# Multiplies behind evictions, loads ordered by need, and a second product in four banks: a fused attention and feed-forward kernel

## The chip, the cores and the metric

The kernel runs on one core of one Trainium2 chip. The metric is the device time of one execution in microseconds, and each kernel has several. An execution counts as slow if it takes over 1.5% longer than the fastest of the same kernel; only fast ones are compared in ratios. The *granted clock* is the mean TensorE clock that the profile records for an execution, 1.00 being full speed. An *eviction* is VectorE's copy of a finished bank of outputs to a buffer, from which a *store* takes it to memory; a *row tile* is 128 tokens of a group.

## The reference, cut to what matters

```python
# q, k, v: [8 batches, 8 heads, 576, 64]
k_p = k.reshape(B, H, 72, 8, D).mean(axis=3)          # 576 rows pooled to 72
v_p = v.reshape(B, H, 72, 8, D).mean(axis=3)
attn = softmax(q @ k_p.T / sqrt(D))
x = (attn @ v_p) -> [4608 tokens, 512]                 # heads side by side
h = x @ w_in                                           # 512 -> 2048, "first product"
out = gelu_tanh(h) @ w_out                             # 2048 -> 512, "second product"
```

The 4608 tokens are done in nine groups of 512. While group g is in its second product, the attention of batch g+1 is worked in between its matmuls.

## The kernel before: the parts that the argument touches

Every product goes to `PS`, eight banks of 512 f32 per partition. Outputs pass through `osb`, a pool of three buffers.

```python
opool = ctx.enter_context(tc.tile_pool(name="op", bufs=3))
PS = psp.tile([128, 8, 512], F32, name="PS")
...
load_k(0, 0, nc.sync)          # the first batch: k and v from SyncE, q from GpSimd
load_k(0, 1, nc.sync)
load_v(0, 0, nc.sync)
load_v(0, 1, nc.sync)
load_q(0, 0)
load_q(0, 1)
...                            # then w_in, batch 1, w_out, all from GpSimd
```

Normalising a head pair takes a logarithm and an exponential on ScalarE and then one or two multiplies on VectorE. The multiplies are issued at once after the exponential, so that they take their place in VectorE's order there:

```python
def norm(b, c, pr, bank):
    ...                        # ld = Ln(sum of the exponentials)
    nc.scalar.activation(out=rc, in_=ld, func=ACT.Exp, scale=-1.0)
    for x in range(2 if b else 1):
        ...
        nc.vector.tensor_tensor(out=xT[rows, pr, col:col + CH], in0=PS[rows, bank + x, :CH],
                                in1=rc[rows], op=ALU.mult)
```

A group: first product with GELU block by block, then the second product, with the next batch's attention steps at fixed places of its 64 matmuls. Two row tiles take turns on banks 0 and 1. In group 0 the order goes by pairs of row tiles, because `w_out` arrives in quarters:

```python
HB = (0, 2, 3, 1)                               # banks of the first product's blocks
...
at = (6, 14, 20, 27, 34, 41, 48, 55, 61)        # places of the attention steps
...                                             # each: score, value, exponential, norm
if g:
    seq = [(r, fo) for r in range(4) for fo in range(FO)]
else:
    for rp in range(2):
        for f4 in range(4):
            seq += [(2 * rp + x, 4 * f4 + f) for x in range(2) for f in range(4)]
for m, (r, fo) in enumerate(seq):
    if m in inserts:
        inserts[m]()
    op = PS[:, r % 2, :]
    nc.tensor.matmul(out=op, lhsT=gT[:, fo, r * 128:(r + 1) * 128], rhs=w_out_b[:, fo, :], ...)
    if fo < FO - 1:
        continue
    osb = opool.tile([128, DM], F32, name="osb")
    nc.vector.tensor_copy(out=osb, in_=op)      # the eviction
    ...                                         # the store, from SyncE
```

The softmax here doesn't subtract the row's maximum and nothing guards it: scores larger than these inputs give would overflow.

Of the kernel before, what the change touches and what calls it, by code (L numbers as in the profile page):

```python
# [8 lines left out]
F32 = mybir.dt.float32  # L9
BF16 = mybir.dt.bfloat16  # L10
ALU = mybir.AluOpType
ACT = mybir.ActivationFunctionType
# [6 lines left out]
def kernel(  # L19
# [9 lines left out]
    nc = tc.nc  # L29
    B, H, S, D = q.shape  # L30
    Sp = S // 8
    N = B * S
    DM = H * D
    DF = moe_w_in.shape[1]
    KO = DM // 128
    FO = DF // 128
    T = S // 32
# [23 lines left out]

    ks, vs, qs = {}, {}, {}

    def load_k(b, hf, eng):
        if b not in ks:
            ks[b] = kvp.tile([KP, 2, KR, 512], F32, name="kt")
        eng.dma_start(
            out=ks[b][:, hf],
            in_=k[b, hf * 4:(hf + 1) * 4].rearrange("h (j r l) d -> (h j) r (l d)", r=KR, l=8))

    def load_v(b, hf, eng):
        if b not in vs:
            vs[b] = kvp.tile([Sp, H, 512], F32, name="vt")
        eng.dma_start(  # L74
            out=vs[b][:, hf * 4:(hf + 1) * 4],
            in_=v[b, hf * 4:(hf + 1) * 4].rearrange("h (j l) d -> j h (l d)", l=8))

    def load_q(b, i):
        if b not in qs:
            qs[b] = qp.tile([128, 2, T * D], BF16, name="qb")  # L80
        nc.gpsimd.dma_start(  # L81
            out=qs[b][:, i],
            in_=q[b, i * 4:(i + 1) * 4].rearrange("h (p t) d -> (h p) (t d)", t=T))

    def load_batch(b):
        for i in range(2):
            load_q(b, i)
        for hf in range(2):
            load_k(b, hf, nc.gpsimd)
        for hf in range(2):  # L90
            load_v(b, hf, nc.gpsimd)

    w_in_b = consts.tile([128, KO, DF], BF16, name="w_in_b")
    w_out_b = consts.tile([128, FO, DM], BF16, name="w_out_b")
# [1 line left out]
    w_out_v = moe_w_out.rearrange("(fo p) d -> p fo d", p=128)  # L96
    identb = consts.tile([128, 128], BF16, name="identb")

    load_k(0, 0, nc.sync)
    load_k(0, 1, nc.sync)  # L100
    load_v(0, 0, nc.sync)
    load_v(0, 1, nc.sync)
    load_q(0, 0)
    load_q(0, 1)
    make_identity(nc, identb)
    for i in range(4):
        nc.gpsimd.dma_start(out=w_in_b[:, :, i * 512:(i + 1) * 512], in_=w_in_v[:, :, i * 512:(i + 1) * 512])

# [86 lines left out]
    def qk(b, c, pr, bank):  # L195
        for e in range(2):
            h = 2 * pr + e
            nc.tensor.matmul(out=PS[:Sp, bank + e, :CH], lhsT=kTs[b % 2][:, c, h, :],  # L198
                             rhs=qTs[b][:, h // 4, h % 4].rearrange("p c t -> p (c t)"),
                             start=True, stop=True)  # L200
# [9 lines left out]
    def av(b, c, pr, bank):  # L210
# [4 lines left out]
        for x in range(2):  # L215
# [3 lines left out]
            else:  # L219
                for y in range(2):  # L220
                    w = vz[:, pr, y] if x else ones[:, y]
                    nc.tensor.matmul(out=PS[:, bank + 1 - x, :CH], lhsT=flat(w), rhs=e[:, y, :],  # L222
                                     start=(y == 0), stop=(y == 1))

    def norm(b, c, pr, bank):
        ld = ep.tile([128, CH], F32, name="ld")
        if b:
            nc.scalar.activation(out=ld[0:64], in_=PS[64:128, bank, :CH], func=ACT.Ln)  # L228
            nc.scalar.activation(out=ld[64:128], in_=PS[0:64, bank + 1, :CH], func=ACT.Ln)  # L229
        else:  # L230
            nc.scalar.activation(out=ld, in_=PS[:, bank + 1, :CH], func=ACT.Ln)
        rc = ep.tile([128, CH], F32, name="rc")
        nc.scalar.activation(out=rc, in_=ld, func=ACT.Exp, scale=-1.0)  # L233
        col = b * S + c * CH
        for x in range(2 if b else 1):
            rows = slice(x * 64, (x + 1) * 64) if b else slice(0, 128)
            nc.vector.tensor_tensor(out=xT[rows, pr, col:col + CH], in0=PS[rows, bank + x, :CH],  # L237
                                    in1=rc[rows], op=ALU.mult)
# [3 lines left out]
    def act_set(name):  # L242
        nc.scalar.preload_act_table_set(name)  # L243


    act_set(EXP_SET)
    for s in k_steps(0, 0):
        s()
    trans_k(0, 0, 4)
    trans_q(0, *QG[0], 5, nc.scalar)  # L250
    trans_q(0, *QG[1], 6, nc.scalar)
    for s in k_steps(0, 1):
        s()
    qk(0, 0, 0, 2), expo(0, 0, 0, 2)
    qk(0, 0, 1, 0), expo(0, 0, 1, 0)
    trans_k(0, 1, 7)
    trans_q(0, *QG[2], 4, nc.vector)
    trans_q(0, *QG[3], 5, nc.vector)
    qk(0, 1, 0, 2), expo(0, 1, 0, 2)
    qk(0, 1, 1, 0), expo(0, 1, 1, 0)  # L260
    for hf in range(2):
        for s in v_steps(0, hf):
            s()
    for c in range(2):
        for pr in (2, 3):
            bank = (2, 0)[pr % 2]
            qk(0, c, pr, bank), expo(0, c, pr, bank)
    for i, (c, pr) in enumerate(ORDER):
        bank = (4, 6, 0, 2, 4, 6, 4, 6)[i]
        av(0, c, pr, bank)  # L270
        norm(0, c, pr, bank)


    HB = (0, 2, 3, 1)
    for g in range(NG):
        r0 = g * GROUP
        nb = g + 1 if g + 1 < B else None
        act_set(GELU_SET)
        if g + 2 < B:
            load_batch(g + 2)  # L280


        side = {fo: [] for fo in range(FO)}
        if nb is not None:
            k0, k1 = k_steps(nb, 0), k_steps(nb, 1)
            v0, v1 = v_steps(nb, 0), v_steps(nb, 1)
            tq = [lambda a=a, i=i: trans_q(nb, *a, 4 + i, nc.vector) for i, a in enumerate(QG)]
            tk = [lambda hf=hf: trans_k(nb, hf, 4 + hf) for hf in range(2)]
            if g:
                plan = {2: k0[:2], 3: k0[2:], 4: tq[:1], 5: [k1[0], tq[1]], 6: k1[1:] + [tq[2]],  # L290
                        7: tq[3:], 9: tk, 10: v0[:1], 11: v0[1:], 12: v1[:1], 13: v1[1:]}
            else:
                plan = {8: tq[:1], 9: [tq[1]], 10: [tq[2]], 11: tq[3:] + k0 + k1, 14: tk,
                        15: v0 + v1}
            for fo, what in plan.items():
                side[fo] += what

        gT = gpool.tile([128, FO, GROUP], BF16, name="gT")

        def p1_mm(fo, ko, c0, c1):  # L300
            nc.tensor.matmul(out=PS[:, HB[fo % 4], c0:c1], lhsT=w_in_b[:, ko, fo * 128:(fo + 1) * 128],  # L301
                             rhs=xT[:, ko, r0 + c0:r0 + c1], start=(ko == 0), stop=(ko == KO - 1))

        def gelu(fo):
            nc.scalar.activation(out=gT[:, fo, :], in_=PS[:, HB[fo % 4], :], func=ACT.Gelu_apprx_tanh)  # L305
            for s in side[fo]:
                s()


        for c0, c1 in ([(0, CH), (CH, GROUP)] if g == 0 else [(0, GROUP)]):  # L310
            for ko in range(KO):
                for fo in range(4):
                    p1_mm(fo, ko, c0, c1)
        for fo in range(4):
            gelu(fo)
        for fo in range(4, FO):
            for ko in range(KO):
                p1_mm(fo, ko, 0, GROUP)
            gelu(fo)


        inserts = {}
        if nb is not None:
            act_set(EXP_SET)
            at = (6, 14, 20, 27, 34, 41, 48, 55, 61)
            for i in range(len(ORDER) + 1):
                def step(i=i):
                    if i < len(ORDER):
                        qk(nb, *ORDER[i], 2)
                    if i:  # L330
                        av(nb, *ORDER[i - 1], 4 + 2 * ((i - 1) % 2))
                    if i < len(ORDER):
                        expo(nb, *ORDER[i], 2)
                    if i:
                        norm(nb, *ORDER[i - 1], 4 + 2 * ((i - 1) % 2))
                inserts[at[i]] = step
        if g:
            seq = [(r, fo) for r in range(4) for fo in range(FO)]
        else:
            seq = []  # L340
            for rp in range(2):
                for f4 in range(4):
                    seq += [(2 * rp + x, 4 * f4 + f) for x in range(2) for f in range(4)]
        for m, (r, fo) in enumerate(seq):
            if m in inserts:
                inserts[m]()
            op = PS[:, r % 2, :]
            nc.tensor.matmul(out=op, lhsT=gT[:, fo, r * 128:(r + 1) * 128], rhs=w_out_b[:, fo, :],  # L348
                             start=(fo == 0), stop=(fo == FO - 1))
            if fo < FO - 1:  # L350
                continue
            osb = opool.tile([128, DM], F32, name="osb")
            nc.vector.tensor_copy(out=osb, in_=op)  # L353
            c0, c1 = r0 + r * 128, r0 + (r + 1) * 128
            while c0 < c1:
                n = min(c1, (c0 // CH + 1) * CH) - c0
                b, c = divmod(c0, S)
                nc.sync.dma_start(
                    out=out[b * S:(b + 1) * S].rearrange("(j e) d -> e j d", e=2)[c // CH, c % CH:c % CH + n],
                    in_=osb[c0 - r0 - r * 128:c0 - r0 - r * 128 + n, :])  # L360
                c0 += n


# [28 lines left out]
```

## Time and profile before

| | before |
|---|---|
| time, median of 3 runs | 351.21 us (350.79 to 351.3) |
| profiled span, granted clock | 348.0 us, 0.958 |
| TensorE busy | 310.6 us |
| TensorE's first product waiting for output evictions | 14.3 us, in 8 waits |
| first GELU starts | 29.77 us |
| group 0's second product | 44.04 to about 66.5 us |

The prediction shows the lines behind most of these. Two more views matter later. The first is busy time by stretch, for the first two slices of 8.7 us; the columns are the stretch, its length, the busy time and number of instructions of TensorE, its weight loads, VectorE, ScalarE and GpSimd, the granted clock, the share of the DMA engines and what they moved in GB/s.

```profile
0.00:8.70 8.70, 0.42 (x3) 0.21 (x3) 3.93 (x10) 1.28 (x1) 7.58 (x16) 1.00 0.82 209
8.70:17.40 8.70, 6.13 (x40) 4.50 (x40) 6.99 (x14) 5.58 (x10) 2.94 (x6) 1.00 1.16 252
```

With both issuers at work, the second slice moved 252 GB/s. The second view is the output stores issued between 50 and 90 us, and the time from issue to landing.

```profile
L358 SPq DMA_DIRECT2D out_dram<-osb x5: 341/368/422, 55.5 to 69.5; - x5
...
DMA to landing us min/median/max: 6.9/8.7/11.5
```

Over the whole kernel the larger group of stores has a median of 2.0 us from issue to landing. Around the end of group 0, where the loads of later batches are in flight, it is 8.7.

### The profile page before, as it was taken

The page shows a single profiled execution, that of the slowest core. Times are in us where ns is not written, and L with a number is a line of the kernel's source. Part 1 is how long each engine was busy: PE and PEld are TensorE (multiplying, and loading weights), DVE is VectorE, ACT ScalarE, POOL GpSimd, SP SyncE. Part 2 cuts the span into 40 slices and gives each one's busy share as a digit, 9 for nine tenths or more (in the row PEclk, how much of TensorE's full clock was granted, in tenths as well). Part 3 has the DMA queues.
Part 4 walks back from the last instruction along what each step waited for, and adds up shares of the span by engine and source line. Part 5 has one row for each costly group of instructions (what it writes and reads, how often), then busy time and mean ns, then how long its engine had stood idle before and what let it go on. Part 6 is the DMA issues. An engine that isn't in the chain of part 4 may idle for free.

```text
span 348.0 us, 4327 instructions
## 1 busy us (share of the span) xinstructions
PE 310.6 (89%) x1601; PEld 157.5 (45%) x1632; DVE 182.5 (52%) x336; ACT 221.6 (64%) x411; POOL 37.0 (11%) x62
## 2 busy tenths in 40 slices
PE   0789897799997999799979997999799979999995
PEld 0555453344553555355535553545354534444442
DVE  4860884558364846584657567575667560020011
ACT  1684474846894689668946796669857985603600
POOL 8332222002100210021002100000000000000000
PEclk9978998989998999999989999899999998999998
DMA  8999999967720583158412851001100110012011
GB/s 209 252 227 223 222 208 177 250 198 176 177 79 32 121 183 127 32 107 184 119 52 40 206 157 61 1 2 44 47 32 0 30 62 30 0 61 62 0 49 72
DMA packets 17228, 37.50 MB, mean 108 GB/s; under 512 B 2328, under 2 KB 6424, under 8 KB 17208
## 3 DMA queue, kind: packets, MB, share of 16 engines
q0 software_dynamic: 11008, 25.44, 34.9%
q1 hardware_dynamic: 6200, 11.80, 10.5%
q8 instruction: 12, 0.20, 0.2%
q14 instruction: 8, 0.07, 0.1%
HBM read 36.70 MB, written 9.44 MB: 133 GB/s over the span
## 4 chain that ended last, share of the span: by engine, by line
PE 80%; DVE 8%; ACT 7%; DMA 2%; issue 1%; DVEq 0%; ACTq 0%; POOLq 0%
PE PS L301 37%; PE PS L348 32%; PE PS L198 4%; PE PS L217 3%; PE PS L181 3%; DVE xT L237 2%; DMA qb<-in_q_dram 2%; DVE osb L353 2%; ACT ld L229 2%; ACT rc L233 2%; ACT e L204 2%; ACT ld L228 1%; DVE vt L138 1%; PE PS L222 1%; DVE kt L138 1%
## 5 line engine op out<-in xcount | busy, mean ns | idle before, releaser
L301 PE MATMUL PS<-xT,w_in_b 128*128 128x512 bf16 (+2 forms) x575 | 143.5, 396 | 15.9 <-DVE osb L353 14.3
L348 PE MATMUL PS<-w_out_b,gT 128*128 128x512 bf16 x562 | 135.2, 381 | 2.9 <-DVE osb L353 2.4
L305 ACT ACTIVATE gT<-PS 128x512 bf16<-128x512 f32 x144 | 82.3, 600 | 81.2 <-PE PS L301 80.1
L301 PEld LDWEIGHTS <-w_in_b 128*128 128x128 bf16 x592 | 59.5, 103 | 83.1 <-issue 30.5
L237 DVE TENSOR_TENSOR xT<-PS,rc 64x288 bf16<-64x288 f32 (+1 forms) x120 | 54.5, 455 | 63.6 <-ACT rc L233 37.4
L348 PEld LDWEIGHTS <-gT 128*128 128x128 bf16 x576 | 56.4, 98 | 60.2 <-issue 4.3
L353 DVE COPY osb<-PS 128x512 f32<-128x512 f32 x36 | 24.8, 692 | 53.1 <-PE PS L348 52.3
L204 ACT ACTIVATE e<-PS 72x576 bf16<-72x576 f32 x64 | 40.8, 645 | 13.8 <-PE PS L198 13.0
L188 DVE COPY qT<-PS 128x640 bf16<-128x640 bf16 (+1 forms) x30 | 22.4, 765 | 31.8 <-PE PS L181 31.7
L138 DVE TENSOR_TENSOR vt<-vt 72x1024 f32<-72x1024 f32 (+1 forms) x32 | 30.5, 952 | 0.8
L233 ACT ACTIVATE rc<-ld 128x288 f32<-128x288 f32 x64 | 28.3, 442 | 2.5 <-DVE xT L237 0.5
L198 PE MATMUL PS<-qT,kT 128*72 128x288 bf16 x128 | 26.8, 298 | 2.5 <-ACT qT L186 1.0
L138 DVE TENSOR_TENSOR kt<-kt 96x768 f32<-96x768 f32 (+1 forms) x32 | 24.0, 749 | 3.7 <-DMA kt<-in_k_dram 3.1
L228 ACT ACTIVATE ld<-PS 64x288 f32<-64x288 f32 x56 | 22.8, 408 | 1.4
L229 ACT ACTIVATE ld<-PS 64x288 f32<-64x288 f32 x56 | 22.5, 402 | 1.4
L217 PE MATMUL PS<-e,vp 72*128 72x288 bf16 x112 | 23.3, 288 | 0.0
L243 ACT ACT_TABLE_LOAD x17 | 21.8, 1283 | 1.0 <-PEq L376 0.7
L198 PEld LDWEIGHTS <-kT 128*72 128x72 bf16 x128 | 14.8, 117 | 16.0 <-issue 2.4
L81 POOL DMA_DIRECT2D qb<-in_q_dram x16 | 9.2, 581 | 106.0 <-PE PS L181 95.2
L171 DVE COPY kT<-PS 64x288 bf16<-64x288 bf16 x32 | 14.4, 450 | 6.5 <-PE PS L168 6.0
L74 POOL DMA_DIRECT2D vt<-in_v_dram x14 | 10.5, 756 | 40.1 <-DVE vp L138 25.8
L181 PEld LDWEIGHTS <-qb 128*128 128x128 bf16 x144 | 11.2, 104 | 7.6 <-DMA qb<-in_q_dram 1.0
(32 smaller groups left out, 80.9 us busy)
## 6 DMA issues: line engine op xcount, KB each, us to landing
kt<-in_k_dram POOLq DMA_DIRECT2D x14, 576.0 KB, 9.0
vt<-in_v_dram POOLq DMA_DIRECT2D x14, 576.0 KB, 8.6
out_dram<-osb SPq DMA_DIRECT2D x24, 256.0 KB, 2.0
qb<-in_q_dram POOLq DMA_DIRECT2D x16, 288.0 KB, 7.0
w_in_b<-in_moe_w_in_dram POOLq DMA_DIRECT2D x4, 512.0 KB, 16.0
w_out_b<-in_moe_w_out_dram POOLq DMA_DIRECT2D x4, 512.0 KB, 20.9
out_dram<-osb SPq DMA_DIRECT2D x8, 192.0 KB, 2.2
kt<-in_k_dram SPq DMA_DIRECT2D x2, 576.0 KB, 5.9
```

Source lines behind the costliest of these rows:

```text
L138: nc.vector.tensor_tensor(out=o, in0=a, in1=b, op=ALU.add)
L198: nc.tensor.matmul(out=PS[:Sp, bank + e, :CH], lhsT=kTs[b % 2][:, c, h, :], rhs=qTs[b][:, h // 4, h % 4].rearrange("p c t -> p (c t)"), st ...
L204: nc.scalar.activation(out=e, in_=PS[:Sp, bank:bank + 2, :CH], func=ACT.Exp, scale=1.0 / 64.0)
L217: nc.tensor.matmul(out=PS[:, bank + x, :CH], lhsT=flat(vps[b % 2][:, pr, x]), rhs=e[:, x, :], start=True, stop=True)
L228: nc.scalar.activation(out=ld[0:64], in_=PS[64:128, bank, :CH], func=ACT.Ln)
L229: nc.scalar.activation(out=ld[64:128], in_=PS[0:64, bank + 1, :CH], func=ACT.Ln)
L233: nc.scalar.activation(out=rc, in_=ld, func=ACT.Exp, scale=-1.0)
L237: nc.vector.tensor_tensor(out=xT[rows, pr, col:col + CH], in0=PS[rows, bank + x, :CH], in1=rc[rows], op=ALU.mult)
L301: nc.tensor.matmul(out=PS[:, HB[fo % 4], c0:c1], lhsT=w_in_b[:, ko, fo * 128:(fo + 1) * 128], rhs=xT[:, ko, r0 + c0:r0 + c1], start=(ko == ...
L305: nc.scalar.activation(out=gT[:, fo, :], in_=PS[:, HB[fo % 4], :], func=ACT.Gelu_apprx_tanh)
L348: nc.tensor.matmul(out=op, lhsT=gT[:, fo, r * 128:(r + 1) * 128], rhs=w_out_b[:, fo, :], start=(fo == 0), stop=(fo == FO - 1))
L353: nc.vector.tensor_copy(out=osb, in_=op)
```

## The change

Its intent: (1) an eviction should not stand in VectorE's order behind a multiply that is not ready, and the bank that is evicted last should be needed last; (2) the first batch's loads go in one queue in the order of need; (3) 16 half-width matmuls of group 0's first product fill gaps of its attention; (4) group 0's second product keeps four row tiles in four banks and goes by quarters of `w_out`, so that the last quarter is needed late, with all eight score steps of batch 1 moved ahead of it.

The core of the diff. Cut are helpers, renamings and three smaller parts: groups 1 to 8 take the first matmuls in an order that touches the late bank after six of them; in group 0 the sums of batch 1's k come before the transposes of its q; ScalarE and VectorE take the first batch's four copies of q in another turn.

```diff
-    load_k(0, 0, nc.sync)
-    load_k(0, 1, nc.sync)
-    load_v(0, 0, nc.sync)
-    load_v(0, 1, nc.sync)
-    load_q(0, 0)
-    load_q(0, 1)
+    load_k(0, nc.sync, 0, 1)
+    load_q(0, 0, 1)                 # GpSimd, as all that follow
+    load_k(0, nc.gpsimd, 1, 2)
+    load_q(0, 1, 2)
     make_identity(nc, identb)
+    load_v(0, 0, 4)
+    load_v(0, 4, 8)
...
     def load_batch(b):              # later batches: k, q, v, one DMA each
+        load_k(b, nc.gpsimd)
+        load_q(b)
+        load_v(b)
...
+    def h_bank(g, fo):              # x, y change places from group to group
+        x, y = x_bank(g), 1 - x_bank(g)
+        if fo == 4:
+            return 7
+        return (x, 2, 3, y)[fo if fo < 4 else (fo - 1) % 4]
+    def o_bank(g, r):
+        if g == 0:
+            return (1, 0, 2, 3)[r]
+        return 1 - x_bank(g) if r % 2 == 0 else x_bank(g)
...
+    take = (0, 0, 0, 0, 0, 4, 6, 6)          # first-product matmuls drawn forward
     for i, (c, pr) in enumerate(ORDER):
         av(0, c, pr, bank)
         norm(0, c, pr, bank)
+        mult(0, c, pr, bank)
+        for fo, ko in early[:take[i]]:
+            p1_mm(0, fo, ko, 0, CH)
...
             if g:                            # groups 1 to 7
+                        at(pos[i], norm, *a)
+                        at(min(pos[i] + 9, 65), mult, *a)   # 65: after the last eviction
+            else:
+                for c, pr in ORDER:
+                    scores(nb, c, pr)        # all before the second product
+                for i in range(len(ORDER)):
+                    at(8 + 6 * i, av, *a)
+                    at(8 + 6 * i, norm, *a)
+                    at(min(8 + 6 * i + 8, 65), mult, *a)
...
         else:
-            for rp in range(2):
-                for f4 in range(4):
-                    seq += [(2 * rp + x, 4 * f4 + f) for x in range(2) for f in range(4)]
+            seq = [(r, 4 * f4 + f) for f4 in range(4) for r in range(4) for f in range(4)]
```

## The prediction

> **What bounds the kernel now.** I read the page's busy line and costliest groups first, then the waits, then the stages (busy time by stretch), then the order of time at one group boundary, and last the granted clock in 1 us slices.
>
> The page's first part and its costliest row (the last field is idle time just before, and who ended it):
>
> ```profile
> PE 310.6 (89%) x1601; PEld 157.5 (45%) x1632; DVE 182.5 (52%) x336; ACT 221.6 (64%) x411; POOL 37.0 (11%) x62
> L301 PE MATMUL PS<-xT,w_in_b 128*128 128x512 bf16 (+2 forms) x575 | 143.5, 396 | 15.9 <-DVE osb L353 14.3
> ```
>
> TensorE sets the end. Its own first-product matmuls wait 14.3 us for VectorE's output evictions, eight times. VectorE is half idle, so this is order, not load. The order of time at the boundary from group 2 to group 3:
>
> ```profile
> 139.61 0.81 PE L348 MATMUL PS<-w_out_b,gT 128*128 128x512 bf16 x3
> ...
> 140.26 0.81 PE L301 MATMUL PS<-xT,w_in_b 128*128 128x512 bf16 x3
> ...
> 140.89 0.44 ACT L233 ACTIVATE rc<-ld 128x288 f32<-128x288 f32 x1
> ...
> 141.37 0.94 DVE L237 TENSOR_TENSOR xT<-PS,rc 64x288 bf16<-64x288 f32 x2 [0.39 <-ACT rc L233]
> 142.34 0.69 DVE L353 COPY osb<-PS 128x512 f32<-128x512 f32 x1
> ...
> 143.09 2.96 PE L301 MATMUL PS<-xT,w_in_b 128*128 128x512 bf16 x13 [2.02 <-DVE osb L353]
> ```
>
> The last second-product matmul is issued by 140.26, but its bank's eviction stands behind two multiplies (0.94 us), which stand behind the reciprocal. The fourth matmul of the next group needs that bank, so TensorE stands for 2.02 us. The stages:
>
> ```profile
> core 0: us, PE busy (x) PEld busy (x) DVE busy (x) ACT busy (x) POOL busy (x), PEclk, DMA share, GB/s
> 24.10:44.00 19.90, 17.74 (x103) 10.09 (x104) 8.17 (x15) 10.45 (x18) 5.15 (x8) 0.88 1.13 226
> 44.00:69.50 25.50, 20.73 (x99) 10.31 (x100) 15.38 (x31) 18.31 (x35) 4.45 (x7) 0.93 1.05 210
> 106.40:143.10 36.70, 34.52 (x182) 17.53 (x185) 22.90 (x43) 26.72 (x50) 3.69 (x6) 0.95 0.44 111
> 143.10:178.30 35.20, 32.93 (x181) 17.08 (x184) 22.89 (x43) 26.73 (x50) 3.70 (x6) 1.00 0.48 114
> ```
>
> Two steady groups of the same work: 36.70 us at clock 0.95, 35.20 at 1.00. The slices after the boundary at 106.4 show where the other 1.5 us went:
>
> ```profile
> 107.00:108.00 1.00, 1.00 (x4) 0.40 (x3) 0.93 (x3) 0.00 (x0) 0.00 (x0) 0.59 0.65 246
> 108.00:109.00 1.00, 1.00 (x4) 0.30 (x2) 0.29 (x1) 0.00 (x0) 0.00 (x0) 0.50 0.06 16
> 109.00:110.00 1.00, 1.00 (x4) 0.45 (x3) 0.00 (x0) 0.00 (x0) 0.00 (x0) 0.50 0.06 12
> ```
>
> So a stall is often followed by 3.4 us at half clock: 0.43 us per matmul instead of 0.216. Five such stretches (from 69.6, 107.3, 178.9, 216.5 and 288.1) follow the boundaries; the stalls ending at 143.1 and 251.8 brought none. Group 0 has two further waits, and the start waits for the first half of q (in the chain that ended last, as start, duration, what):
>
> ```profile
> 1.26 7.73 DMA qb<-in_q_dram
> 9.04 0.73 PE PS L181 x5
> ```
>
> ```profile
> 43.03 0.30 PE L168 MATMUL PS<-identb,kp 96*128 96x96 bf16 x3 [1.54 <-DVE kp L138]
> 55.49 0.59 PE L348 MATMUL PS<-w_out_b,gT 128*128 128x512 bf16 x2 [2.44 <-DVE osb L353]
> 67.79 0.81 PE L301 MATMUL PS<-xT,w_in_b 128*128 128x512 bf16 x3 [1.33 <-DVE osb L353]
> ```
>
> **What the Trainium skill says.** "TensorE: Matmul & The Clock Gate", section "What's actually happening": the array's clock is halved after an idle window of about 3.4 us and restored after a busy one, on a free-running window. The trace agrees on the length (3.4 us) and the factor (0.50), but shows that a 2.0 us stall suffices if it lies inside one window: 104.4 to 106.4 was punished, 141.1 to 143.1 was not. The slow stretches begin at multiples of about 3.41 us from one another (107.3 to 178.9 is 21 of them), so which stalls are punished is phase. "Advanced Engine Details and Errata", section "Sequencer Loop": an instruction waits in its engine's queue for its semaphores; the same-order effect is seen above, with the ready eviction 2 us behind a multiply that is not ready. "Perfetto Trace Analysis", section "Matmuls": independent groups should rotate through PSUM banks so that evictions overlap matmuls. Here the next group's fourth matmul takes the bank evicted last, and the 2.02 us show it. "DMA: Bandwidth & Descriptors", section "Issuing engines are not separate DMA queues": all issuers share the same 16 DMA engines. The trace agrees: q took 7.73 us beside k and v from the other queue, against a minimum of 4.0 us from issue to landing for q in this trace.
>
> **The change part by part.**
>
> *Multiplies behind evictions, other bank order (groups 1 to 8).* Same instructions. The last eviction now starts about 0.2 us after the last second-product matmul and takes 0.69, as at 315.86 where no multiply is in front and TensorE resumes 0.95 us after its last issue. The late bank is now touched after six matmuls, 6 x 0.216 = 1.3 us, so the 2.02 us wait goes. The two multiply pairs end about 1.86 and 2.8 us after the product's end; the fifth output block uses bank 7, needed at 16 x 0.216 = 3.45 us, so they don't bind. Groups 2 and 3 read these last columns of xT after 8 and 12 matmuls (1.72, 2.6 us): up to 0.25 us each. A steady group becomes 35.20 - 2.02 = 33.2 us; check: 128 x 0.2155 + 16 pairs of score and value matmuls x 0.245 + 1.3 of transposes = 32.8. Groups 1 to 6 took 217.5 us (69.5 to 287.0): 217.5 - 6 x 33.2 = 18.3 saved, of which about 12 are stalls and the rest half clock. Group 7: 29.6 becomes 27.7 (half clock 1.7, and a 0.3 us wait): 1.9. Group 8: the waits at 317 and 319 go, as bank 7 is free: about 0.5.
>
> *Start.* With v no longer beside it, q's first half should land at about 5.5 to 6.5 instead of 9.0. Transposes then begin about 1.3 us earlier, behind k. But VectorE has one more q copy (0.72) and the same v sums, which still begin near 14.5 (14.91 before), so the last normalisation moves by only about 0.3 us. The real gain is 16 half-width matmuls of group 0's first product drawn into the gaps: before, 32 of them took 24.12 to 30.0, mostly at half clock. I put the first GELU at 26.5 instead of 29.77: 3.3.
>
> *Group 0's middle.* k is summed earlier, which takes away the 1.54 us wait. But all eight score pairs now stand before the second product, and the product's first bank is one of theirs. From the first product's end at about 38.2 (26.5 + 48 x 0.2155 + 1.3): the table load of 1.28 ends about 39.6, eight exponentials x 0.65 = 5.2, so the second product starts at about 44.8, 0.8 us later than before (44.04). TensorE has only 2 us of work in those 6.6, so I expect one half-clock stretch, 1.7 lost. Then 64 x 0.2155 + 8 x 0.245 + 1.7 = 17.5: end at 62.4 against 66.5 before. The stretch is shorter because the score matmuls (8 x 0.245) and the 2.44 us wait no longer lie in it. w_out is no bound: its last quarter landed about 48 (issue 27.4 + 20.9) and is needed 48 positions in, near 58.
>
> *Sum.* Group 0 ends at 62.4; then 6 x 33.2 + 27.7 + 27.6 + 4.0 (last eviction and store, 344.0 to 348.0, unchanged) = 258.5; with 0.4 for groups 2 and 3, 321.3 of span. The timed median is 3.2 us above the profiled span (351.2 against 348.0): 324.5.
>
> **The rivals.** *A new wait in the old one's place:* the next group now waits for the multiplies (bank 7, last columns of xT). Against: the end times above; for: a margin of only 0.65 us at bank 7, and none in groups 2 and 3. If 1 us stayed at each of seven boundaries, about 331; if half clock also stayed, 338 or more. *Group 0 as a new bubble:* the exponentials serialise scores for over 6 us and cost two half-clock stretches, or w_out comes later; about 4 us more, 328. *Loads hidden anyway, or late in one queue:* v behind k and q might reach VectorE after 14.5. By bytes (2.36 MB at 0.25 MB/us from 1.5 us) it lands at about 11 and 14, so at most 1 us is lost: 325.5. *Better than thought:* the clock stays up at start and in group 0: 3 to 4 us less, 321.
>
> **Range and chances.** The steady part (about 20.7 of the 26.7 us) rests on a measured group without stalls, so most uncertainty is in group 0: 324.5, range 319 to 331. Faster by over 2% (below 344.2) needs under a third of the steady gain: 0.97. Within 2%: 0.02. Slower: 0.01, some overlooked serialisation.
>
> **What would show it right or wrong.** The wait of the first product for the output eviction falls from 14.3 us to under 2; steady groups last 33 to 33.5 us at clock 0.99 or more; eight exponentials stand in a row at 39 to 45 with TensorE mostly idle and one slow stretch after; the first GELU stands at 26 to 28; group 0's second product ends between 61 and 65. The prediction is wrong if the boundaries keep a wait above 0.5 us (for a multiply or a GELU), if slow stretches appear inside dense groups, or if the second product of group 0 waits for w_out.

## The result, and the profile after

| | before | after |
|---|---|---|
| time, median of 4 runs | 351.0 us (349.75 to 351.3) | 337.27 us (334.9 to 338.08) |
| ratio of fast runs | | 0.960 (95%: 0.955 to 0.966) |
| profiled span, granted clock | 348.0 us, 0.958 | 336.2 us, 0.968 |

Ratios here and below are the mean time of one kernel's fast runs over that of the other's of the same rounds, so not quite the ratio of the medians quoted. The change is faster by 4%, but the time is 12.8 us above the predicted 324.5 and outside its range.

The profile's first part and the row of the first product, after:

```profile
PE 302.5 (90%) x1601; PEld 155.5 (46%) x1632; DVE 183.0 (54%) x336; ACT 221.2 (66%) x411; POOL 28.7 (9%) x44
...
L265 PE MATMUL PS<-xT,w_in_b 128*128 128x512 bf16 (+2 forms) x575 | 134.2, 379 | 12.2 <-DVE osb L279 11.2
```

The wait for output evictions is 11.2 us where it was 14.3. Read alone, this row says that the change hardly worked. But it was eight waits and is now two, both at one place. First, a steady boundary in order of time, from group 2 to group 3. Each line has start and length in us, engine, line, operation, what is written and read, and the count; brackets give how long the engine was idle before, and what released it.

```profile
144.39 0.81 PE L274 MATMUL PS<-w_out_b,gT 128*128 128x512 bf16 x3
145.04 3.23 PE L265 MATMUL PS<-xT,w_in_b 128*128 128x512 bf16 x13
145.24 0.69 DVE L279 COPY osb<-PS 128x512 f32<-128x512 f32 x1 [1.49 <-PE PS L274]
145.67 0.44 ACT L230 ACTIVATE rc<-ld 128x288 f32<-128x288 f32 x1
145.96 1.88 DVE L238 TENSOR_TENSOR xT<-PS,rc 64x288 bf16<-64x288 f32 x4
```

This is the aim of the change: the eviction starts 0.20 us after the next group's first matmul, the multiplies stand behind it, and 13 matmuls of the next group run without a pause. Now the stages, with the columns of the slices above (group 0's second product, group 1, group 2):

```profile
49.91:65.70 15.79, 15.69 (x78) 7.76 (x80) 8.90 (x19) 11.31 (x25) 0.84 (x1) 1.00 1.11 183
65.70:111.94 46.24, 34.84 (x183) 17.50 (x185) 22.68 (x41) 24.45 (x47) 2.20 (x3) 0.89 0.77 175
111.94:145.04 33.10, 32.88 (x182) 17.10 (x185) 22.90 (x42) 26.71 (x51) 2.20 (x3) 1.00 0.50 122
```

A steady group takes 33.10 us at clock 1.00. Group 1, the same work, takes 46.24 at 0.89, yet its TensorE is busy only 34.84: some 11 us are idle. The order of time where group 0 ends and group 1 begins:

```profile
63.31 0.69 DVE L279 COPY osb<-PS 128x512 f32<-128x512 f32 x1 [1.36 <-PE PS L274]
...
64.03 14.86 SPq L285 DMA_DIRECT2D out_dram<-osb  x5
...
64.99 0.69 DVE L279 COPY osb<-PS 128x512 f32<-128x512 f32 x1
...
66.67 0.69 DVE L279 COPY osb<-PS 128x512 f32<-128x512 f32 x1
67.42 1.24 PE L265 MATMUL PS<-xT,w_in_b 128*128 128x512 bf16 x5 [1.34 <-DVE osb L279]
77.82 0.69 DVE L279 COPY osb<-PS 128x512 f32<-128x512 f32 x1 [10.46 <-DMA out_dram<-osb]
...
78.57 5.01 PE L265 MATMUL PS<-xT,w_in_b 128*128 128x512 bf16 x14 [9.91 <-DVE osb L279]
```

Read the brackets backwards. TensorE stood for 9.91 us until the eviction at 77.82, which stood for 10.46 us until an **output store** had landed. Four row tiles in four banks all finish within the last quarter, so four evictions come in a row, and there are three `osb` buffers. The fourth eviction needs the first one's buffer, whose store was issued at 64.03. The chain that ended last has that store as one piece, and the view of the stores issued between 50 and 90 us shows that it is no exception:

```profile
64.03 13.67 DMA out_dram<-osb
```

```profile
DMA to landing us min/median/max: 8.0/13.7/15.0
```

A store is 128 x 512 x 4 bytes, 0.26 MB. In these 13.67 us the DMA engines moved 184 GB/s, some 2.5 MB, at a busy share of 1.03: they are full of loads for later batches, of which batch 3's were issued from 46.55 to 52.41. The kernel before had slow stores there too (8.7 us median), but its pairs of row tiles gave two evictions at a time, and none of them had to wait for a buffer.

At the start, the loads by slices, the chain's first piece of work, and the line where VectorE begins to sum v:

```profile
0.00:8.70 8.70, 1.03 (x9) 0.82 (x10) 4.39 (x11) 1.28 (x1) 6.59 (x15) 1.00 0.79 189
8.70:17.40 8.70, 5.95 (x35) 3.59 (x33) 5.37 (x8) 5.94 (x10) 5.83 (x8) 1.00 1.10 199
```

```profile
1.26 6.79 DMA qb<-in_q_dram
```

```profile
16.23 1.95 DVE L133 TENSOR_TENSOR vt<-vt 72x1024 f32<-72x1024 f32 x2 [1.43 <-DMA vt<-in_v_dram]
```

The first half of q lands only 0.94 us sooner than before (6.79 against 7.73), 199 GB/s are moved with nearly all loads from one issuer where two issuers moved 252, and v now holds VectorE up until 16.23, where the sums began at 14.91 before without waiting. The next load is later still: q of batch 1, which group 0's first product transposes between its last blocks. Its piece in the chain that ended last, and the transposes that wait for it:

```profile
12.96 26.75 DMA qb<-in_q_dram
```

```profile
39.76 0.45 PE L176 MATMUL PS<-identb,qb 128*128 128x128 bf16 x5 [1.04 <-DMA qb<-in_q_dram]
```

The chain goes through this load and not through the first GELU: an earlier first GELU alone would only have made TensorE wait longer here.

Where the time is, by the prediction's own terms (each end of a stage as predicted and as in the trace, in us):

| stage | predicted | measured | off by | off in sum |
|---|---|---|---|---|
| first GELU | 26.5 | 30.70 | +4.2 | +4.2 |
| group 0's first product ends | 38.2 | 43.40 | +1.0 | +5.2 |
| second product starts | 44.8 | 49.91 | -0.1 | +5.1 |
| second product ends | 62.4 | 65.70 | -1.8 | +3.3 |
| group 1 takes | 33.2 | 46.24 | +13.0 | +16.3 |
| groups 2 to 6 take | 166.4 | 164.71 | -1.7 | +14.7 |
| group 7 takes | 27.7 | 27.63 | -0.1 | +14.6 |
| group 8 and the last store | 31.6 | 31.9 | +0.3 | +14.9 |

Group 1's row has the prediction's steady group, and 166.4 is 5 x 33.2 and the 0.4 for groups 2 and 3. The sum is the difference of the spans, 336.2 against 321.3. The row of the first product's end is set by q of batch 1, as said above, whatever the row before it shows. Of group 1's 13.0 us, 9.91 are the wait for the buffer, 1.34 an eviction of group 0 that still stands behind two multiplies (64.04 and 65.71) and the rest, some 1.7, half clock: the idle stretch brought the clock down from about 72 to 82.4, and the matmuls from 78.57 to 82.4 ran at 0.43 us each instead of 0.216.

### The profile page after: what moved, and what is told of

Same layout as the page of the kernel before. It is cut to its first block, busy times and chain, and to the rows that moved or that the text cites. A ratio compares the mean times of both kernels' runs of the same rounds, so it can differ in the third digit from the quotient of the medians.

```text
span 336.2 us, 4281 instructions
## 1 busy us (share of the span) xinstructions
PE 302.5 (90%) x1601; PEld 155.5 (46%) x1632; DVE 183.0 (54%) x336; ACT 221.2 (66%) x411; POOL 28.7 (9%) x44
## 4 chain that ended last, share of the span: by engine, by line
PE 76%; DMA 14%; ACT 5%; POOL 1%; issue 1%; DVE 1%; DVEq 0%; POOLq 0%
PE PS L265 34%; PE PS L274 33%; DMA qb<-in_q_dram 10%; DMA out_dram<-osb 4%; PE PS L212 4%; PE PS L193 3%; ACT e L199 2%; PE PS L176 2%; ACT ld L226 1%; ACT ld L225 1%; DVE osb L279 1%; ACT rc L230 1%; PE PS L163 0%; ACT L244 0%; POOL kT L120 0%
## 5 line engine op out<-in xcount | busy, mean ns | idle before, releaser
L265 PE MATMUL PS<-xT,w_in_b 128*128 128x512 bf16 (+2 forms) x575 | 134.2, 379 | 12.2 <-DVE osb L279 11.2
L274 PE MATMUL PS<-w_out_b,gT 128*128 128x512 bf16 x562 | 133.7, 379 | 1.2 <-ACT e L199 0.7
L265 PEld LDWEIGHTS <-w_in_b 128*128 128x128 bf16 x592 | 57.2, 99 | 72.7 <-issue 15.3
L183 DVE COPY qT<-PS 128x512 bf16<-128x512 bf16 (+1 forms) x30 | 22.4, 762 | 7.0 <-PE PS L176 6.8
L193 PEld LDWEIGHTS <-kT 128*72 128x72 bf16 x128 | 14.6, 116 | 18.3 <-issue 3.3
L176 PE MATMUL PS<-identb,qb 128*128 128x128 bf16 x144 | 13.9, 231 | 1.4 <-DMA qb<-in_q_dram 1.4
L176 PEld LDWEIGHTS <-qb 128*128 128x128 bf16 x144 | 11.2, 104 | 8.5 <-DMA qb<-in_q_dram 2.1
L68 POOL DMA_DIRECT2D kt<-in_k_dram x8 | 5.1, 634 | 112.0 <-DVE kp L133 104.3
## 6 DMA issues: line engine op xcount, KB each, us to landing
qb<-in_q_dram POOLq DMA_DIRECT2D x7, 576.0 KB, 11.2
```

Of the source, the lines that this page charges most:

```text
L176: nc.tensor.transpose(out=half_bank(bank)[:, x * 128:(x + 1) * 128], in_=qs[b][:, i, (t0 + x) * 128:(t0 + x + 1) * 128], identity=identb)
L193: nc.tensor.matmul(out=PS[:Sp, bank + e, :CH], lhsT=kTs[b % 2][:, c, h, :], rhs=qTs[b][:, h // 4, h % 4].rearrange("p c t -> p (c t)"), st ...
L265: nc.tensor.matmul(out=PS[:, h_bank(g, fo), c0:c1], lhsT=w_in_b[:, ko, fo * 128:(fo + 1) * 128], rhs=xT[:, ko, r0 + c0:r0 + c1], start=(ko ...
L274: nc.tensor.matmul(out=PS[:, o_bank(g, r), :], lhsT=gTs[g][:, fo, r * 128:(r + 1) * 128], rhs=w_out_b[:, fo, :], start=(fo == 0), stop=(fo ...
```

## The experiments

Two questions: is the buffer the cause of group 1's length, and what is the cause of the start's? Each expectation says which theory it speaks for, by letters; A is the theory of the buffers just told. Twelve kernels ran, in four batches, each batch on one chip; all gave correct results. The edits shown leave out helper parameters. The kernel before has medians of 349.5 to 349.9 in these batches, but single runs from 343.4 (granted clock 0.99) to 352.1 (0.95). As the fastest run sets the mark, many runs of before count as slow in three of the batches, and the verdicts of the first batch are unclear, presumably for that reason, in spite of their intervals. Differences between versions are therefore read from their own runs, which mostly agree within 3 us (four runs each, six of g2 and g3).

| run | median us (lowest to highest) | ratio to before (95%) |
|---|---|---|
| e1_four_out | 326.05 (324.43 to 329.03) | 0.943 (0.928 to 0.959) |
| e2_pairs | 333.45 (330.73 to 337.2, one slow) | 0.961 (0.944 to 0.978) |
| e3_v_sync | 328.19 (327.15 to 329.34) | 0.949 (0.939 to 0.958) |
| e4_steady_only | 327.43 (326.9 to 328.03) | 0.946 (0.937 to 0.955) |
| f1_filler | 328.7 (327.68 to 328.99) | no interval |
| f2_no_early | 328.16 (327.21 to 329.38) | no interval |
| f3_old_loads | 327.44 (326.86 to 328.7) | no interval |
| f4_steady_g0 | 323.27 (323.06 to 323.41) | no interval |
| g1_hold | 329.95 (327.25 to 334.83, one slow) | 0.941 (0.935 to 0.948) |
| g2_f4_four_out | 322.64 (321.52 to 323.85) | 0.923 (0.919 to 0.928) |
| g3_best_filler | 321.01 (320.04 to 322.25) | 0.918 (0.914 to 0.923) |
| h1_loads_filler | 322.72 (322.08 to 322.98) | no interval |

### Is it the buffer? e1_four_out

The kernel after, with one more output buffer and nothing else.

```diff
-    opool = ctx.enter_context(tc.tile_pool(name="op", bufs=3))
+    opool = ctx.enter_context(tc.tile_pool(name="op", bufs=4))
```

> The changed kernel with four output buffers instead of three, nothing else. Theory A (the fourth store of group 0 has no free output buffer until the first store, 13.7 us in flight, lands): VectorE's wait for the output store (10.5 us) goes, the 9.9 us wait of TensorE and the half clock after it (1.6 us) go: about 326 us. Rival B (the evictions are late because the multiplies and evictions stand in the wrong order in group 0, and the buffer is only what the profile names last): the wait moves to a multiply or an eviction and the time stays above 333.

Measured: 326.05 us, 11.2 below the kernel after. The same place in order of time:

```profile
66.64 1.29 DVE L279 COPY osb<-PS 128x512 f32<-128x512 f32 x2
67.38 2.97 PE L265 MATMUL PS<-xT,w_in_b 128*128 128x512 bf16 x13 [1.33 <-DVE osb L279]
```

The third and fourth evictions run one after the other (x2, 1.29 us), the wait for a store is gone, and only the 1.33 us remain. The stores are not faster: those between 50 and 90 us have a median landing of 13.6 us. Only nobody waits for them. Everything before 65.7 is as in the kernel after (first GELU 30.64, second product 49.88 to 65.7), so this run also separates the two causes.

### From the other side: e2_pairs

The kernel after with its three buffers, but group 0's second product in pairs of row tiles, as before.

```diff
-            seq = [(r, 4 * f4 + f) for f4 in range(4) for r in range(4) for f in range(4)]
+            seq = [(2 * rp + x, 4 * f4 + f) for rp in range(2) for f4 in range(4)
+                   for x in range(2) for f in range(4)]
```

> The changed kernel with three output buffers, but group 0's second product in pairs of row tiles (rows 0 and 1 through all of w_out, then 2 and 3). Theory A: the first store is now issued about 7 us earlier, so its 13.7 us end near 71 instead of 77.7 and the fourth eviction waits about 4 us instead of 10.5: about 331 us. Rival B (order of multiplies and evictions at the end of group 0): no shorter wait, 337. A third possibility is that a quarter of w_out is late for the pairs, seen as a wait for w_out.

Measured: 333.45 us with a wide spread; the three fast runs are 330.73, 331.26 and 335.64, so two of them meet the expected 331. VectorE's wait for a store shrinks from 10.5 to 5.2 us (expected 4), and TensorE's wait behind it to 4.6: the first two evictions come early, so that the oldest store has had longer. A wait of 0.6 us for `w_out` appears, which going by quarters had avoided. Pairs alone halve the wait; they don't remove it, as the first store, issued at 56.72, takes 14.12 us here, where the slowest one of the kernel before took 11.5.

### Take away what the store waits behind: g1_hold

The kernel after with three buffers. The loads of batch 3 are held back until the last multiply of batch 1, by a small GpSimd copy that reads its output ahead of them in the queue.

```diff
+        if g == 1:
+            hold = consts.tile([64, 1], BF16, name="hold")
+            nc.gpsimd.tensor_copy(out=hold, in_=xT[0:64, 3, 2 * S - 1:2 * S])
         if g + 2 < B:
             load_batch(g + 2)
```

> The changed kernel with its three output buffers; only the loads of batch 3 (first used in group 2) are held until the last multiply of batch 1, by one small GpSimd copy that reads what it wrote. Theory A in full (the buffer is only late because its store stands in the DMA engines behind loads that nobody needs yet): the first store lands within 8 us instead of 13.7, VectorE's wait for it falls from 10.5 to 5 or less, and the time to 327 to 332. Rival G (stores are slow at that point for a reason of their own, such as SyncE's queue or writing): the landing time stays above 12 and the time at 337.

Measured: 329.95 us; its fast runs are 327.25 to 330.5. The wait for a store is gone although there are three buffers; the stores between 50 and 90 us now take 7.0 us in the median and 10.7 at most, against 13.7 and 15.0. So the wait has two causes that must come together: too few buffers for four evictions, and stores that share the DMA engines with loads issued far ahead. Taking either away removes it.

### The start: is it v's place in the queue? e3_v_sync

A caution first. Up to the start of group 0's second product, after, e1, e2 and g1 are the same code, and yet their traces have the first GELU at 30.70, 30.64, 28.97 and 32.48, and the second product at 49.91, 49.88, 47.99 and 51.53. One trace's place of the first GELU is therefore good to about 2 us only; the times of all runs weigh more.

e3 is e1 with the first batch's v loaded from SyncE again.

```diff
-    load_v(0, 0, 4)
-    load_v(0, 4, 8)
+    load_v(0, 0, 4, nc.sync)
+    load_v(0, 4, 8, nc.sync)
```

> Four output buffers as in the first run, and v of the first batch issued from SyncE's queue again. Theory C (one queue alone moves fewer bytes per us than two together, so v, w_in, then k and q of the second batch land late): v lands 3 us or more earlier, k and q of the second batch 2 to 4 us earlier, no wait for q inside group 0's first product, and 2 to 4 us less than the first run: 322 to 324. Rival D (all queues share the same engines, so the order alone counts): within 1 us of the first run, with q's first half later by as much as v is earlier.

Measured: 328.19 us, a miss, 4 to 6 us above what was expected and no better than e1. q's first half comes later (the transposes begin at 9.90 instead of 8.37 in e1), the sums of v begin at 17.22 and not earlier, the first GELU at 32.1. The wait for q of batch 1 in group 0's first product is gone, as expected, so that its last GELU is at 43.53 (43.32 in e1) in spite of the later first one; but a half-clock stretch from 47 to 54 meets the second product. The place of v alone is not the cause.

### All loads as before: f3_old_loads

e1 with every load in the order and the queue that the kernel before has.

```diff
     load_k(0, nc.sync, 0, 1)
+    load_k(0, nc.sync, 1, 2)
+    load_v(0, 0, 4, nc.sync)
+    load_v(0, 4, 8, nc.sync)
     load_q(0, 0, 1)
-    load_k(0, nc.gpsimd, 1, 2)
     load_q(0, 1, 2)
     make_identity(nc, identb)
-    load_v(0, 0, 4)
-    load_v(0, 4, 8)
     # later batches: q, k, v in halves
```

> The four-buffer version with all loads in the order and queues of the kernel before (k and v of the first batch by SyncE, q in front of k in later batches, halves). Theory C (late k and q of the second batch hold group 0): no wait for q at 39.7, k of the second batch lands at 33 to 36; but q's first half is later, so the first GELU is at 31 to 32; in all within 2 us of the four-buffer version. If the new load order brings what it was made for, 2 us or more slower.

Measured: 327.44 us, within 2 us of e1 as expected; first GELU 30.60 (30.64 in e1), though v is summed from 15.86. The second product starts sooner, at 49.06, as nothing waits for q of batch 1, but a half-clock stretch from 45.5 to 53 lies in it. The loads alone don't explain the start either, and the new load order brings nothing that these runs show.

### Is it the clock? f1_filler

The granted clock column reads 1.00 in both early slices above. The value matmuls (exponentials times v, and times ones for their sums) run mostly later. From 18 to 27 us the column reads 0.50 in the kernel after; in e1 it reads 1.00 there, but the durations are the same. The same 16 value matmuls (288 columns), in the kernel before and in e1, by form over the first 40 us (busy us, mean ns of one; 407 ns in the kernel after):

```profile
L222 PE MATMUL PS<-e,ones 72*128 72x288 bf16 x16 | 3.7, 320 | 0.2 <-ACT ld L231 0.2
```

```profile
L217 PE MATMUL PS<-e,ones 72*128 72x288 bf16 x16 | 5.4, 439 | 0.0
```

Their starts lie 0.24 us apart in e1 and 0.12 apart at full speed. f1 is e1 with matmuls on a tile of zeros in TensorE's early gaps, into banks not yet in use:

```diff
+    fz = consts.tile([128, 512], BF16, name="fz")
+    nc.vector.memset(fz, 0.0)
...
+    def filler(n, bank):
+        for _ in range(n):
+            nc.tensor.matmul(out=PS[:, bank, :], lhsT=fz[:, 0:128], rhs=fz, start=True, stop=True)
     act_set(EXP_SET)
+    filler(11, 0)
     ...                             # and 3, 4 and 4 more, up to the value matmuls
```

> The four-buffer version with filler matmuls on zeros (128 x 512, result never read) put into the gaps of TensorE's first 17 us, so that its clock is up while the first batch's value matmuls run. Theory E (the start failed because TensorE ran it at half clock, 0.24 us for each 288-column matmul, so that the value matmuls and not ScalarE set the pace): the value matmuls go at 0.12 us, and the first GELU comes at about 27 to 28 instead of 30.6. The time falls by at most 1 us, because q of the second batch lands near 39.7 and holds the chain there. Rival F (late loads set the first GELU): it stays at 30 or later.

Measured: 328.7 us, above e1 and not up to 1 us below it: a miss. The value matmuls take 310 ns in the mean instead of 439, so filling brings the clock up for some of them, but the first GELU comes only to 29.54 (expected 27 to 28), within the spread of the same code. v still lands late (its sums begin at 15.68 and 19.05), TensorE waits 1.94 us for q of batch 1 until 39.50 (1.07 until 39.73 in e1: the earlier GELU became waiting), and half clock comes from 23.5 to 27 and from 40.5 to 44 instead, so that the second product starts at 51.31. The clock alone is not the cause.

### Loads and clock together: h1_loads_filler

f3 with fillers: loads as before, clock kept up.

```diff
+    filler(12, 0)
     for s in k_steps(0, 0):
         s()
     trans_k(0, 0, 4)
+    filler(3, 7)
     trans_q(0, *QG[0], 5, nc.scalar)
     trans_q(0, *QG[1], 6, nc.vector)
+    filler(4, 7)
     ...                             # and 3 and 2 more
```

> The four-buffer version with the loads of the kernel before (first GELU at 30.6 there, value matmuls at half clock) and filler matmuls in TensorE's gaps of the start. Theory E with C (the prediction's first GELU at 26.5 failed because it took the value matmuls at full clock and v as early as in the kernel before; the matmuls drawn forward do pay once both hold): value matmuls near 0.12 us, first GELU at 26.5 to 28, time 324 to 326 against 327.4 without fillers. Rival H (the matmuls drawn forward delay the last normalisations whatever the clock is): first GELU at 29.5 or later, time unchanged.

Measured: 322.72 us (expected 324 to 326), 4.7 below f3 and 3.3 below e1; the ranges of the runs lie apart. The value matmuls and the first GELU:

```profile
L222 PE MATMUL PS<-e,ones 72*128 72x288 bf16 x16 | 3.3, 286 | 0.0
```

```profile
25.97 3.54 ACT L276 ACTIVATE gT<-PS 128x512 bf16<-128x512 f32 x7
```

The first GELU stands at 25.97 (predicted 26.5), the second product starts at 44.58 (predicted 44.8) and ends at 61.8 (predicted 62.4). So the start has two constraints side by side, the loads and the clock. Removing one leaves the other: f1 and f3 gained nothing over e1, both together 3.3 us. The loads here are v and q of batch 1 together; a run that repairs the clock and only one of these was not made.

### What the single parts are worth: e4_steady_only, f4_steady_g0, f2_no_early

e4 is the kernel before with only the multiplies behind the evictions and the bank order of groups 1 to 8 (the start, the loads and group 0 as before, but that in group 0 banks 0 and 1 change places).

```diff
+                        if g:
+                            behind.setdefault(min(at[i] + 9, 65), []).append(a)
+                        else:
+                            mult(*a)
...
-            op = PS[:, r % 2, :]
+            op = PS[:, o_bank(g, r), :]
```

> The kernel before with only the multiplies behind evictions and the bank order of groups 1 to 8; start, loads and group 0 as before. If the steady part gives what was predicted (five further boundaries without 2.0 us wait and without half clock after it, 17.1 us in groups 1 to 6, 1.9 in group 7, 0.5 in group 8), the span falls from 348.0 by 19.5 to 328.5 and the time to about 331.5, faster than the whole change (337). If the gain of the steady part was overestimated, 335 or more.

Measured: 327.43 us, 4 better than the expected 331.5. A part of that is the wait from group 0 to group 1, which fell too (1.32 and 0.24 us, without half clock, against 1.33 and 0.89 with 3.4 us of it in before). This small part is 10 us better than the whole change.

f4 adds group 0's multiplies to it, still with pairs of row tiles, three buffers and the old start.

```diff
-                        if g:
-                            behind.setdefault(min(at[i] + 9, 65), []).append(a)
-                        else:
-                            mult(*a)
+                        behind.setdefault(min(at[i] + 9, 65), []).append(a)
```

> The kernel before with only the multiplies behind evictions, in group 0 too, and the bank order of groups 1 to 8; loads, start and group 0's pairs of rows as before, three output buffers. The 2.44 us wait inside group 0 goes, with it the half clock after it (1.7), and most of the 1.3 at its end: 3 to 5 us less than the same without group 0 (327.4), so 322 to 324, faster than the whole change with four buffers (326). Rival: the pairs' evictions then wait for an output buffer (third store within 14 us): 326 or more.

Measured: 323.27 us, as expected, with all four runs within 0.35 us. Group 0's second product runs from 43.98 to 62.3, with the scores inside it; in e1 the stretch from the first product's end to the second's is 43.3 to 65.7. That is 18.3 against 22.4 us. By these two traces, which differ in the order of row tiles too, drawing the scores ahead costs 4 us, as TensorE is busy for only 3.51 of the 6.51 us beside the eight exponentials. Even here the fourth eviction waits for a buffer, only more briefly:

```profile
64.21 0.69 DVE L378 COPY osb<-PS 128x512 f32<-128x512 f32 x1 [2.14 <-DMA out_dram<-osb]
```

f2 is e1 without the 16 matmuls drawn forward; they come in front of the others of group 0.

```diff
-    take = (0, 0, 0, 0, 0, 4, 6, 6)
+    take = (0, 0, 0, 0, 0, 0, 0, 0)
```

> The four-buffer version without the 16 matmuls drawn forward between the value matmuls; they come after the last of these. If drawing them forward pays (the prediction's 3 us), the first GELU is later by 2 to 4 us. If TensorE is at half clock and so fully used there, the two orders take the same time: the last multiply comes 2 us earlier, the first GELU within 1 us of 30.6, and the time within 1 us of the four-buffer version.

Measured: 328.16 us; the first GELU is at 32.86, 2.2 later than in e1, and the second product starts 1.0 later. That looks like the gain of drawing forward, but in this trace the sums of v already begin 2.1 us later (18.30 against 16.24), which the edit doesn't touch. From there to the first GELU it is 14.56 us against 14.40. So at half clock no gain is shown, as the second expectation had it, and the times (327.21 to 329.38 against 324.43 to 329.03) leave the question open. Its value matmuls run almost unbroken from 21.6 to 28.6, 0.24 us each: seven us of such matmuls did not bring the clock up.

### A version that beats both: g2_f4_four_out and g3_best_filler

g2 is f4 with four output buffers. g3 is g2 with fillers (12, 3, 4, 3 and 2) and the last k transposes of batch 1 moved behind group 0's last block.

```diff
-    opool = ctx.enter_context(tc.tile_pool(name="op", bufs=3))       # g2
+    opool = ctx.enter_context(tc.tile_pool(name="op", bufs=4))
...
-                plan = {8: tq[:1], 9: [tq[1]], 10: [tq[2]], 11: tq[3:] + k0 + k1, 14: tk,    # g3
-                        15: v0 + v1}
+                plan = {8: tq[:1], 9: [tq[1]], 10: [tq[2]], 11: tq[3:] + k0 + k1,
+                        15: tk + v0 + v1}
```

> The version with steady part and group 0's multiplies behind evictions (323.3), with four output buffers. That version's fourth eviction in group 0 waited 2.1 us for a store and TensorE 1.2 us for it; these go: 1 to 1.5 us less, about 322. If the wait is only moved to the next multiply, no change.

> As the version before, with filler matmuls at the start that keep TensorE's clock up, and group 0's k transposes moved behind its last first-product block. Theory E (half clock sets the pace of the start, ScalarE would otherwise): value matmuls at 0.12 us, last logarithm of batch 0 at about 24, first GELU at 27 to 28.5 instead of 29.7, and 1.5 to 3 us less in all: 319 to 321. If the loads set group 0's pace: first GELU earlier, but the time unchanged.

Measured: 322.64 and 321.01 us, six runs each. g2 lies 0.6 below f4, but in another batch and with overlapping runs; its trace shows no wait at the boundary. In g3 the first GELU moves from 29.35 to 27.82, and part of that is lost to new waits for `w_out`, 0.41 and 0.79 us. g3 is the fastest kernel, 1.6 us below g2 in the same batch, 8% below before and about 16 us below the kernel after.

## Why the prediction was wrong

**Right: the steady boundary.** It said that a steady group would become 33.2 us and keep no wait above 0.5 us. Groups 2 to 6 last 32.9 us in the mean (164.71 / 5) at clock 1.00, and no wait for a multiply stayed; the rival of a new wait in the old one's place fell. e4 alone, with 327.4 us, shows that this part carries the gain.

**The step that failed first: group 0's end, in the sum of "group 0 ends at 62.4; then 6 x 33.2".** It counted TensorE's work and the exponentials, and asked whether `w_out` comes in time (it does; the kernel after shows no such wait). It treated group 1 as a steady group and had no term for the output buffers. Going from two banks to four turned two and two evictions into four in a row against three buffers, and the stores in flight there last 13.67 us instead of 2. That made 9.91 us of wait and brought 1.7 of half clock; e1 and g1_hold show both halves of the cause. The rival "group 0 as a new bubble" had the place, but named the exponentials and `w_out`. The 1.34 us are a second miss: in group 0 the multiplies are only eight places behind their step, so two of them still come between the last evictions.

**The second: the start, "the first GELU at 26.5".** One term was too small and two were missing. v was to land "at about 11 and 14", worked out from 0.25 MB per us; its sums began at 16.23 and 19.31. That rate was the kernel before's with two issuers; at the 189 and 199 GB/s of the kernel after the same bytes would land at about 12.3 and 15.3 (an estimate from these two slices), so the rate explains some 1.3 us. By 16.23 the engines had moved some 3.1 MB (same slices) and not the 2.36 MB counted, so loads issued behind v moved beside it. The start has no term for the speed of the value matmuls, which in before ran at full clock up to about 21.9 us; here they ran at half clock. Nor has it one for q of batch 1. It landed at 39.7, and by the order of the matmuls a first GELU at 26.5 would only have lengthened the wait for it, as in f1. (The "one more q copy" on VectorE is a misreading: it has two of the four before and after.) h1, which takes all loads back to the old order and fills the gaps, meets the predicted 26.5, 44.8 and 62.4 within 0.6 us each. So the part of the change that was to help here, the one queue in the order of need, did not.

**Sizes.** The middle of group 0 was right in sum (6.6 us predicted, 6.51 measured), with some luck: the table load ended 1.84 us after the first product and not 1.4, and the eight exponentials took 4.61 us and not 5.2. The half-clock stretch expected after it did not come in the kernel after, so that the second product took 15.8 us and not 17.5; it did come in e3, f2, f3, g1 and h1, so whether it comes is not steady. Group 7 (27.63) and the end (31.9) were right. The prediction's text takes 1.9 and 0.5 us off groups 7 and 8, its sum only 1.7 off the 61.0 us that both took before (287.0 to 348.0); so its steady part is 19.6 us in its own sum (18.3 + 1.7 - 0.4), and not 20.7.

**Where the missing gain went.** Of the 14.9 us, 11.7 turned into a new wait for the output buffer with its half clock, 1.3 into the eviction behind multiplies, and 5.1 were never there up to the second product; 3.5 came back as the absent half clock and in groups 2 to 6, the rest being roundings. The 4 us of the score steps ahead of the second product are no error of the prediction, which counted them, but they need not be paid: f4, which leaves out all parts but the multiplies and the banks, is 14 us faster than the kernel after.

**Still open.** What decides the clock in the first 20 us is not settled: f3 and the kernel before have the same loads and nearly the same matmuls, and yet the value matmuls take 427 ns in f3 and 320 in before; filling raises it, but the exact condition was not isolated. Nor was it shown why f2's v landed 2 us later, or why single runs of before differ by up to 8 us in one batch; their granted clocks differ with them.

## What to carry to other kernels

When a change lets more tiles finish together, count the buffers that they leave through, and how long one of these is held *at that place* of the trace, not in the median: a store behind prefetched loads can last several times longer. Then read a wait through to its last releaser, as a wait "for an eviction" may be one for a store. Finally, check the clock by the duration of one kind of matmul, and expect two constraints side by side where removing one brings nothing.

## What the Trainium skill lacked or had wrong

- "DMA: Bandwidth & Descriptors", section "Queues, rings and completion order", says that each DMA engine takes packets in turn from the queues that it has work for. Alone, that lets one expect that a 0.26 MB store gets its share quickly. Here it took 13.67 us (8.0 to 15.0 among its neighbours) beside loads queued from GpSimd, and 2.1 us in the median over the kernel. The page has no figure for a store among prefetched loads.
- "TensorE: Matmul & The Clock Gate", section "What's actually happening", gives an idle window for the throttle and a busy one for its release, but not how much work makes a window busy. In f2, seven us of value matmuls with 72 rows, almost unbroken, did not release it (0.24 us each); in the kernel before, 2.0 us of idleness within a window sufficed to throttle.
- No page says that the granted clock can read 1.00 from the start of an execution while the matmuls run at half speed: so it does in e1 up to 28 us (value matmuls of 439 ns against 286 in h1), where the kernel after reads 0.50 from 18 to 27 (407 ns).
- No page says that one issuer can move less than two at the start of a kernel: 189 and 199 GB/s in the first two slices here and 189 and 208 in e1, against 209 and 252 in before and 204 and 253 in f3 with both.
